# One add moves from VectorE to the head of GpSimd's string of adds

## The chip, the cores and the metric

The kernel runs on one core of a Trainium2 chip. The metric is the device time of one execution in microseconds (us), the median of three runs. Engine names in the profile: PE is TensorE's matrix product, PEld its weight load, DVE is VectorE, ACT is ScalarE, POOL is GpSimd, SP is SyncE, which here only issues transfers. L906 is line 906 of the kernel.

## What is computed

```python
# x: 8 x 4096 x 192, weight: 8 heads x 7 taps, w_in: 192 x 2048, w_out: 2048 x 192, all float32
w = softmax(weight)                                     # over the 7 taps of each head
idx = np.arange(S)[:, None] + np.arange(K)[None, :]
x_unf = x_pad[:, idx, :].reshape(B, S, K, H, group)     # x_pad: 6 zeros ahead of each sequence
x = np.einsum('hk,bskhg->bshg', w, x_unf).reshape(B * S, D)
h = x @ w_in
g = h * (1.0 / (1.0 + np.exp(-1.702 * h)))
out = g @ w_out
```

So each of the 32768 tokens gets a weighted sum of itself and its six predecessors (the convolution, seven taps), and then a two-layer network with the activation `g`.

## The kernel before, in words

**Chunks and periods.** The tokens are worked through in 32 chunks of 1024 (`N_BIG`), numbered `big`. After a first chunk of its own form, each chunk has a first product, conv(x) @ w_in (function `hidden`, line 775), and a second product, g @ w_out (function `second`, line 1154). I call one first product with the second product behind it a period. Both products use a scheme in which sums and differences of blocks are multiplied instead of the blocks themselves, so that fewer products are needed and many adds are. In the trace, TensorE's matmuls of the first product stand at L709 (164 of them in a period, 41 terms of four) and those of the second at L1172 (some 624).

**The order is written by hand.** `HIDDEN` (line 737) is a list of steps of the first product, `PLAN` (line 1108) one of the second. A program walks through a list and issues each step at once; the step goes to the end of its engine's queue. Each engine works through its queue in order and waits by semaphore where an operand isn't ready or a place is still being read. So the place of a step in the list decides what it stands behind on its own engine. In `HIDDEN`, "mm" is a term on TensorE, "copy" and "gelu" move or activate a bank of results (engine "a" is ScalarE, "v" VectorE), "join" adds two results on VectorE, "tap" makes the next tap on ScalarE, "add" adds taps, "over", "ve", "vl" make sums of convolved blocks on GpSimd (L435, L437) and "vc", "over" and "vl" issue their copies across the two halves of the partitions on SP (L609). In `PLAN`, "go" issues matmuls, "join" adds on VectorE (L435, L437), "turn" transposes a finished result on VectorE (L1091), and "acc" is an accumulating transfer issued by GpSimd (L1148).

**The taps.** The convolution of a chunk is made ahead, from the second product two chunks before to the first product one chunk before. Its 192 columns form three groups c = 0, 1, 2. From the fourth chunk on, ScalarE makes all 21 taps (line 570): `x` shifted by k, times weight k, 128 x 512 values each, every one into a place of its own (`tap_home`), k = 0 straight into the sum's place (`own`). The places are parts of buffers that are free just then, mostly of `g`. Taps 1 and 5 of group 2 use the same place, as do taps 3 and 6. The list "ready" holds the taps in the order c = 1, 0, 2; eighteen are issued in `PLAN`, the last three (c = 2, k = 4, 5, 6) in `HIDDEN`, of which k = 4 stands at the very start of the first product.

**The adds of the taps.** The taps of groups 0 and 1 are summed by accumulating transfers on GpSimd's queue (L595), with four last adds on GpSimd, "fin 0" to "fin 3". Those of group 2 are summed by six adds of 128 x 512 values, "c2 1" to "c2 6"; the number is that of the tap that is added. In `tap`, line 572 chooses what a tap is added to:

```python
base = tap_home(big, c, 2) if k in (3, 4) else dst
```

So taps 3 and 4 are added to tap 2, and tap 2 with both, tap 1, tap 5 and tap 6 to the sum. The step ("add", engine, name) in `HIDDEN` issues one of them if its tap has been made (line 906 for either engine). GpSimd's queue holds, in order: "c2 1", "fin 0", "fin 1", "fin 2", "c2 2", "fin 3", "c2 5", "c2 6", and then the sums of "vl" 19, "over", "ve" 0 and "vl" 15. VectorE's queue holds "c2 3" between two pairs of copies out of PSUM and "c2 4" behind the second pair. "c2 2" waits for "c2 4". This is done in 29 of the periods.

Of the kernel before, what the change touches and what calls it, by code (L numbers as in the profile page):

```python
# [15 lines left out]
def kernel(  # L16
# [101 lines left out]
    g = consts.tile([P, NG, 2, 2, NG, T], F32)  # L118
# [80 lines left out]
    def own(big):  # L199
        return conv_t[:, big % 2 * NR : big % 2 * NR + NR, :]  # L200
# [156 lines left out]
    for c in range(NC):  # L357
        part = sel[:, c, :].rearrange("i (h q) -> i h q", h=2)
        for sign in (1, -1):
# [5 lines left out]
                base=R * c if sign == 1 else group - 1 - R * c,  # L365
# [170 lines left out]
    def tap_home(big, c, k):  # L536
        if big == 1:
            return homes_1[c][k - 1]
        if big < 3:
            return (first_taps if c == 0 else taps[3])[k - 1]  # L540
        return taps[c][k - 1]

    def conv_src(big, c, k, ns=slice(0, 2)):
        return xts[big][:, c, ns, Q - PAD + k : Q - PAD + k + T]

    def conv(big, c, k, ns=slice(0, 2), times=vec.tensor_scalar_mul):
        src = conv_src(big, c, k, ns)
        dst = own(big)[:, 2 * c + ns.start : 2 * c + ns.stop, :]
        tap = cw[:, c, k : k + 1]
        if k == 0:  # L550
            times(dst, src, tap)
        else:
            vec.scalar_tensor_tensor(
                out=dst, in0=src, scalar=tap, in1=dst, op0=ALU.mult, op1=ALU.add
            )
# [10 lines left out]
    def tap(big, c, k):  # L566

        dst = own(big)[:, 2 * c : 2 * c + 2, :]
        home = tap_home(big, c, k) if k else dst
        act.mul(home, conv_src(big, c, k), cw[:, c, k : k + 1])  # L570
        if k and c not in DMA_TAPS and big > 2:
            base = tap_home(big, c, 2) if k in (3, 4) else dst
            to_add[f"c{c} {k}"] = base, home
            add_homes(big, c, k)
            return
        if big > 2:
            add_homes(big, c, k)
            if (c, k) == (0, K - 1):
                for i, (b, j, n) in enumerate(FINAL):
                    out, src = (tap_home(big, b, q) if q else own(big)[:, 2 * b : 2 * b + 2, :] for q in (j, n))  # L580
                    to_add[f"fin {i}"] = out, src
            return
        homes = [dst] + [tap_home(big, c, i) for i in range(1, K)]
        for a, b in (PAIRS_1 if big == 1 and c == 0 else TREE).get(k, ()):
            tree.append((homes[a], homes[b]))
        end_taps(2 if big == 2 and (c or k == K - 1) else 0)
# [3 lines left out]
    def add_homes(big, c, k):  # L590
        for b, i, j in LATER.get((c, k), ()) if big > 2 else ():
            out, src = (
                tap_home(big, b, n) if n else own(big)[:, 2 * b : 2 * b + 2, :] for n in (i, j)
            )
            nc.gpsimd.dma_start(out=out, in_=src, accum_op=ALU.add)  # L595

    def end_taps(left=0):
        while len(tree) > left:
            out, src = tree.pop(0)
            nc.gpsimd.dma_start(out=out, in_=src, accum_op=ALU.add)  # L600
# [96 lines left out]
    def prepare_taps(big):  # L697

        for c in (0, 2) if big < 3 else (1, 0, 2):
            for k in range(K):  # L700
                yield "", 1.0, lambda c=c, k=k: tap(big, c, k)
        yield f"taps {big}", 0.0, lambda: None
# [29 lines left out]
    def plain(u, m, n, v, slot, ks=range(NC), first=0):  # L732
# [2 lines left out]
            product1(slot, NC * (2 * u + m) + k, 2 * k + n, 0, v, k == first)  # L735

    HIDDEN = [
# [693 lines left out]
    for big in range(1, N_BIG):  # L1431
        more = big + 1 < N_BIG
        hidden(big, tiles, work)
        f, x, a, y = (tiles[i] for i in NEXT)
# [37 lines left out]
```

## Time and profile before

| | us |
|---|---|
| median of 3 runs (2297.59 to 2299.92) | 2299.07 |
| the profiled execution, its own time | 2295.66 |
| its span, from the first to the last instruction | 2293.9 |
| TensorE busy | 2258.6 |
| VectorE busy | 2158.2 |
| ScalarE busy | 1715.2 |
| GpSimd busy | 919.4 |

The busy times are those of the span of 2293.9. The granted clock of TensorE is 0.999 of full speed over the span. In the rows of the profile, "room<-room,slot" names the output's tile and then the inputs' tiles; `slot` and `sums` lie in PSUM, all others in SBUF (`out_dram` and `in_x_dram` in HBM). "96x256" is partitions by elements. In a timeline a row gives start and length in us, the engine, the line, the operation, and in brackets the engine's idle time before it and what ended that. In the waits a row gives who waited for whom, the total, the times and the longest. Rows of several equal instructions are merged (x2).

### The profile page before, as it was taken

The numbers are of one execution on the slowest core, as the hardware profiler recorded it, in microseconds if no ns is written. First come the engines' busy times: TensorE is split into PE (matmuls) and PEld (weight loads), VectorE is DVE, ScalarE is ACT, GpSimd is POOL, SyncE is SP. The second block draws the span as 40 slices with busy tenths as digits, with TensorE's granted clock in tenths as the row PEclk, the third lists the DMA queues.
The fourth block names the chain that finished last, engine by engine and source line by source line (L and its number), as shares of the span: only waits on it lengthen the run. The fifth ranks groups of instructions, "written<-read, shape, count | busy, mean of one in ns | idle before, by whom it ended". The sixth has DMA issues, their size and how long they took to land.

```text
span 2293.9 us, 63896 instructions
## 1 busy us (share of the span) xinstructions
PE 2258.6 (98%) x25090; PEld 1342.3 (59%) x25090; DVE 2158.2 (94%) x3297; ACT 1715.2 (75%) x3335; POOL 919.4 (40%) x980
## 2 busy tenths in 40 slices
PE   9999999999999999999999999999999999999999
PEld 5356566656566756666555555555555555657754
DVE  8999999999999999999999999999999999999998
ACT  8767777777877777777777677777777777777744
POOL 1534444334543344443345433354334444334510
PEclk9999999999999999999999999999999999999999
DMA  9986678766778767787666876668866768765643
GB/s 203 160 171 141 136 143 161 154 129 141 142 155 160 141 135 146 142 163 151 134 140 131 161 158 137 133 137 157 162 140 134 148 134 166 153 134 112 136 97 70
DMA packets 341995, 329.66 MB, mean 144 GB/s; under 512 B 131648, under 2 KB 280768, under 8 KB 341696
## 3 DMA queue, kind: packets, MB, share of 16 engines
q0 software_dynamic: 66352, 167.47, 41.4%
q1 hardware_dynamic: 273696, 157.72, 30.0%
q8 instruction: 199, 3.26, 0.6%
q14 instruction: 100, 0.82, 0.1%
q10 hardware_dynamic: 1648, 0.39, 0.1%
HBM read 53.15 MB, written 25.17 MB: 34 GB/s over the span
## 4 chain that ended last, share of the span: by engine, by line
PE 86%; DVE 7%; DMA 3%; issue 2%; ACT 2%; POOL 0%; SPq 0%; ACTq 0%; DVEq 0%; POOLq 0%
PE slot L709 34%; PE slot L1172 25%; PE sums L1172 15%; PE sums L709 12%; DVE room L435 2%; DVE room L437 1%; DVE g L437 1%; DMA w_form<-w_form 1%; DVE osbs L1091 1%; DMA g<-g 1%; DMA w_out_s<-w_form 0%; DMA g<-osbs 0%; ACT room L1201 0%; ACT room L1197 0%; DMA w_form<-w_out_s 0%
## 5 line engine op out<-in xcount | busy, mean ns | idle before, releaser
L709 PE MATMUL slot<-conv_t,w_in_s 64*128 64x512 f32 x3372 | 865.7, 593 | 4.3 <-DMA conv_t<-conv_t 1.4
L1172 PE MATMUL slot<-g,w_form 128*32 128x256 f32 x5872 | 716.9, 379 | 0.4 <-ACT slot L1201 0.4
L709 PEld LDWEIGHTS slot<-conv_t,w_in_s 64*128 64x128 f32 x3372 | 455.3, 187 | 295.7 <-issue 182.4
L437 DVE TENSOR_TENSOR g<-g 128x1024 f32<-128x1024 f32 x372 | 443.5, 1219 | 25.2 <-ACT g L833 18.4
L1172 PE MATMUL sums<-g,w_form 128*32 128x256 f32 x3800 | 422.2, 379 | 0.0
L1172 PEld LDWEIGHTS slot<-g,w_form 128*32 128x32 f32 x5872 | 362.1, 110 | 90.6 <-ACT slot L1201 0.9
L709 PE MATMUL sums<-conv_t,w_in_s 64*128 64x512 f32 x1284 | 379.5, 592 | 0.6 <-DMA conv_t<-conv_t 0.3
L826 ACT ACTIVATE g<-slot 128x512 f32<-128x512 f32 x494 | 266.2, 624 | 124.9 <-PE slot L709 124.6
L1172 PE MATMUL slot<-g,w_out_s 128*32 128x256 f32 x4080 | 321.8, 380 | 22.0 <-DVE room L435 20.9
L1197 ACT COPY room<-slot 32x256 f32<-32x256 f32 x434 | 158.9, 366 | 212.5 <-PE slot L1172 203.2
L1148 POOL DMA_DIRECT2D g<-g x124 | 116.0, 936 | 455.1 <-PE slot L1172 348.9
L906 POOL TENSOR_TENSOR conv_t<-conv_t,g 128x512 f32<-128x512 f32 x174 | 229.2, 1333 | 132.5 <-DVE g L906 105.0
L437 POOL TENSOR_TENSOR conv_t<-conv_t 128x256 f32<-128x256 f32 x210 | 181.8, 882 | 235.1 <-PE slot L709 89.6
L570 ACT ACTIVATE g<-xt,cw 128x512 f32<-128x512 f32 x389 | 270.3, 719 | 4.4
L1172 PEld LDWEIGHTS slot<-g,w_out_s 128*32 128x32 f32 x4080 | 164.1, 110 | 154.2 <-DVE room L435 30.1
L1172 PEld LDWEIGHTS sums<-g,w_form 128*32 128x32 f32 x3800 | 210.8, 110 | 69.7
L709 PEld LDWEIGHTS sums<-conv_t,w_in_s 64*128 64x128 f32 x1284 | 176.8, 187 | 108.3 <-issue 66.0
L833 ACT ACTIVATE g<-g 128x1024 f32<-128x1024 f32 x155 | 170.2, 1098 | 2.0 <-DVE g L817 1.9
L709 PE MATMUL slot<-g,w_in_s 64*128 64x512 f32 x556 | 170.6, 591 | 0.2 <-DVE slot L817 0.2
L1197 ACT COPY room<-sums 32x256 f32<-32x256 f32 x217 | 79.5, 366 | 105.4 <-PE sums L1172 95.9
L826 ACT ACTIVATE g<-sums 128x512 f32<-128x512 f32 x188 | 104.5, 615 | 58.4 <-PE sums L709 57.6
L1172 PE MATMUL sums<-g,w_out_s 128*32 128x256 f32 x1872 | 146.0, 380 | 0.1
(243 smaller groups left out, 3895.0 us busy)
## 6 DMA issues: line engine op xcount, KB each, us to landing
g<-g POOLq DMA_DIRECT2D x124, 512.0 KB, 6.5
conv_t<-conv_t SPq DMA_DIRECT2D x844, 64.0 KB, 2.0
xin<-in_x_dram SPq DMA_DIRECT2D x240, 180.0 KB, 6.4
out_dram<-osbs SPq DMA_DIRECT2D x186, 128.0 KB, 2.5
g<-g POOLq DMA_DIRECT2D x66, 256.0 KB, 6.5
g<-g SPq DMA_DIRECT2D x248, 64.0 KB, 3.5
g<-room POOLq DMA_DIRECT2D x31, 512.0 KB, 6.1
g<-osbs POOLq DMA_DIRECT2D x30, 512.0 KB, 6.4
```

The costliest lines, as they stand in the source:

```text
L435: eng.tensor_add(v(dst), v(a), v(b))
L437: eng.tensor_sub(v(dst), v(a), v(b))
L570: act.mul(home, conv_src(big, c, k), cw[:, c, k : k + 1])
L709: nc.tensor.matmul(slot[h], w_in_s[halves[h], a, v * P : (v + 1) * P], src, start=first, stop=True, skip_group_check=True,)
L826: act.activation(dst[:, :, h, :], ot(bank(src, h)), AF.Gelu_apprx_sigmoid, scale=float(sign))
L833: act.activation(dst.rearrange("p o h t -> p h o t"), src, AF.Gelu_apprx_sigmoid, scale=float(sign))
L906: (vec if eng == "v" else nc.gpsimd).tensor_add(dst, dst, home)
L1091: vec.transpose(osb[:, n, js, m * Q : (m + 1) * Q], src)
L1148: nc.gpsimd.dma_start(out=spot(dst), in_=spot(a), accum_op=ALU.add)
L1172: nc.tensor.matmul(dst, w, t, start=first, stop=last, skip_group_check=True)
L1197: act.copy(to, d)
```

## The change

Two places of the kernel are edited. Tap 4 of group 2 is now added to tap 1, no longer to tap 2; and this add goes from VectorE to GpSimd and stands in `HIDDEN` right behind the step in which ScalarE makes tap 4, ahead of "c2 1". The sum is that of the same seven taps.

```diff
         if k and c not in DMA_TAPS and big > 2:
-            base = tap_home(big, c, 2) if k in (3, 4) else dst
+            base = tap_home(big, c, {3: 2, 4: 1}[k]) if k in (3, 4) else dst
             to_add[f"c{c} {k}"] = base, home
...
     HIDDEN = [
-        ("mm", 0, 8, 1, 1), ("tap",), ("add", "g", "c2 1"), ("add", "g", "fin 0"), ("add", "g", "fin 1"),
-        ("mm", 0, 0, 2, 1), ("copy", "a", "k0", "p1", 1), ("mm", 0, 2, 3, 1), ("copy", "v", "k4", "p0", 1),
-        ("copy", "a", "k5", "p2", 1), ("mm", 0, 16, 1, 0), ("add", "v", "c2 3"), ("add", "g", "fin 2"),
-        ("copy", "a", "k6", "p3", 1), ("mm", 1, 13, 0, 0), ("copy", "v", "k2", "p1", 1), ("mm", 0, 3, 2, 0),
-        ("copy", "a", "k3", "p0", 1), ("add", "v", "c2 4"), ("mm", 0, 13, 3, 0), ("copy", "v", "k1", "p2", 1),
+        ("mm", 0, 8, 1, 1), ("tap",), ("add", "g", "c2 4"), ("add", "g", "c2 1"), ("add", "g", "fin 0"),
+        ("add", "g", "fin 1"), ("mm", 0, 0, 2, 1), ("copy", "a", "k0", "p1", 1), ("mm", 0, 2, 3, 1),
+        ("copy", "v", "k4", "p0", 1), ("copy", "a", "k5", "p2", 1), ("mm", 0, 16, 1, 0), ("add", "v", "c2 3"),
+        ("add", "g", "fin 2"), ("copy", "a", "k6", "p3", 1), ("mm", 1, 13, 0, 0), ("copy", "v", "k2", "p1", 1),
+        ("mm", 0, 3, 2, 0), ("copy", "a", "k3", "p0", 1), ("mm", 0, 13, 3, 0), ("copy", "v", "k1", "p2", 1),
         ("add", "g", "c2 2"), ("add", "g", "fin 3"), ("copy", "a", "p0", "k6", -1), ("mm", 0, 6, 1, 0),
```

The number and the order of all other steps stay as they are. On GpSimd's queue the string becomes "c2 4", "c2 1", "fin 0", "fin 1", "fin 2", "c2 2", "fin 3", "c2 5", "c2 6", with "c2 4" waiting for ScalarE's tap 4; "c2 2" now waits for "c2 3" alone.

## The prediction

> **What bounds the kernel now.** I read the page first, for which engine is full, then TensorE's waits, then a table of whole periods, and last the rows of each engine around the one wait that counts.
>
> ```profile
> span 2293.9 us, 63896 instructions
> PE 2258.6 (98%) x25090; PEld 1342.3 (59%) x25090; DVE 2158.2 (94%) x3297; ACT 1715.2 (75%) x3335; POOL 919.4 (40%) x980
> ```
> ```profile
> PE slot L1172 <- DVE room L435: 20.9, 19, 1.3
> ```
> TensorE is busy for 98% of the span and VectorE for 94%; GpSimd has room. Nothing that leaves TensorE's work alone can bring much more than TensorE's own gaps. In the waits of PE one line stands out: 19 waits of about 1.1 us (20.9 in all) for an add of VectorE in the second product. How much time such a wait costs is seen from periods. A period runs from one chunk's first product to the next; the table of windows has 28 periods together, the one period before them, three first products alone, and two whole periods (columns: length, busy time and instructions of each engine, granted clock, share of the DMA engines, GB/s).
>
> ```profile
> 248.92:2219.54 1970.62, 1950.86 (x22068) 1174.57 (x22064) 1864.68 (x2798) 1487.66 (x2894) 821.85 (x863) 1.00 0.72 143
> 177.55:248.92 71.37, 70.07 (x792) 47.18 (x788) 67.95 (x100) 53.96 (x104) 31.22 (x33) 1.00 0.75 149
> 600.62:636.26 35.64, 35.64 (x169) 19.50 (x165) 34.25 (x52) 28.46 (x52) 16.77 (x17) 1.00 0.55 122
> 951.47:987.11 35.64, 35.64 (x168) 26.79 (x164) 34.45 (x52) 28.47 (x52) 17.14 (x18) 1.00 0.52 117
> 530.59:566.81 36.22, 36.22 (x168) 26.17 (x165) 35.40 (x52) 29.11 (x53) 16.57 (x17) 1.00 0.55 122
> 882.03:951.47 69.44, 69.44 (x792) 44.04 (x788) 65.57 (x100) 53.45 (x104) 28.37 (x31) 1.00 0.74 148
> 1022.20:1092.96 70.76, 69.66 (x792) 47.86 (x788) 67.34 (x101) 53.45 (x104) 29.39 (x32) 1.00 0.73 146
> ```
> A period without a gap takes 69.44 us, with TensorE busy from end to end at the full clock (1.00). One with the gap takes 70.76, 1.32 more. So 69.44 is the floor and the change can only win the gaps. Where the 1.32 comes from is in the timeline ahead of the first product that starts at 1022.20 (start, length, engine; then VectorE, GpSimd and TensorE in turn):
>
> ```profile
> 1017.17 0.42 DVE L435 TENSOR_TENSOR room<-room 96x256 f32<-96x256 f32 x1
> 1017.51 2.11 DVE L437 TENSOR_TENSOR room<-room 96x256 f32<-96x256 f32 x1
> 1019.55 0.43 DVE L1091 STREAM_TRANSPOSE osbs<-room 96x256 f32<-96x256 f32 x1
> 1019.91 0.37 DVE L435 TENSOR_TENSOR room<-room,slot 96x256 f32<-96x256 f32 x1
> ```
> ```profile
> 1017.16 0.86 POOL L595 DMA_DIRECT2D conv_t<-g  x1 [2.35 <-DMA g<-g]
> 1017.73 1.60 POOL L906 TENSOR_TENSOR conv_t<-conv_t,g 128x512 f32<-128x512 f32 x1
> 1020.03 1.28 POOL L906 TENSOR_TENSOR conv_t<-conv_t,g 128x512 f32<-128x512 f32 x1 [0.70 <-DMA g<-room]
> 1021.27 2.64 POOL L906 TENSOR_TENSOR g<-g 128x512 f32<-128x512 f32 x2
> ```
> ```profile
> 1018.89 0.38 PE L1172 MATMUL slot<-g,w_form 128*32 128x256 f32 x1
> 1020.34 0.42 PE L1172 MATMUL slot<-g,w_out_s 128*32 128x256 f32 x3 [1.07 <-DVE room L435]
> ```
> A subtraction of VectorE with both inputs in SBUF (room<-room), whose like takes 0.42, takes 2.11: it ends at 1019.62, 0.29 after GpSimd's add (1017.73 + 1.60 = 1019.33). That add is "c2 1", GpSimd's first of the period. Everything behind on VectorE is 1.7 us late, the join room<-room,slot among it, which TensorE then awaits until 1020.34. Beside it the same place of the clean period that begins at 882.03:
>
> ```profile
> 878.63 0.42 DVE L437 TENSOR_TENSOR room<-room 96x256 f32<-96x256 f32 x1
> ```
> ```profile
> 879.19 1.61 POOL L906 TENSOR_TENSOR conv_t<-conv_t,g 128x512 f32<-128x512 f32 x1
> ```
> Here "c2 1" starts 0.14 after the subtraction has ended, nothing is held, and no gap follows. So the gap is a collision: an add of GpSimd holds a VectorE operation whose inputs are both in SBUF.
>
> **The change part by part.** What moves is GpSimd's whole string of adds. Its new first member, "c2 4", needs the tap that ScalarE makes at the head of the first product:
>
> ```profile
> 1022.75 0.72 ACT L570 ACTIVATE g<-xt,cw 128x512 f32<-128x512 f32 x1
> ...
> 1028.81 1.33 ACT L570 ACTIVATE g<-xt,cw 128x512 f32<-128x512 f32 x2
> ```
> The first row is that tap (k=4), done at 1023.47; the second is taps 5 and 6. GpSimd works in order, so "c2 1", "fin 0" and "fin 1" behind "c2 4" cannot start before 1023.5. Between 1018 and 1023.5 GpSimd then has no add to run, and the subtraction at 1017.51 has nobody to be held by. That removes the gap in each of the 19 periods that have it.
>
> The sum of that, from the windows: 28 periods take 1970.62 against 28 x 69.44 = 1944.32, so 26.3 us lie above the floor. The period before them (71.37) ends with such a gap too, worth 1.3 by the longest wait: 27.6 together. Some 25 of it are the 19 gaps (19 x 1.32 = 25.1), the rest are late starts in the first product. These have the same origin: the last join, room<-room at 1023.15, is held by "fin 2" (GpSimd's second add of the row at 1021.27):
>
> ```profile
> 1023.15 1.04 DVE L435 TENSOR_TENSOR room<-room 96x256 f32<-96x256 f32 x1
> ...
> 1025.77 0.67 DVE L906 TENSOR_TENSOR g<-g 128x512 f32<-128x512 f32 x1
> ```
> After the change it starts at the same 1023.15 (it follows TensorE's last product), takes 0.42 and is over at 1023.57, about when "c2 4" begins. VectorE's two copies and its remaining add "c2 3" come 0.6 us earlier, "c2 3" at about 1025.1.
>
> What the change adds, first on VectorE. "c2 4" (0.67) goes, but "c2 3" has both inputs in SBUF and now meets GpSimd: "c2 4" runs from 1023.5 to 1024.8, "c2 1" from 1024.8 to 1026.1. So "c2 3" is held until about 1026.1 and ends near 1026.6 instead of 1026.4. The trace has this case already:
>
> ```profile
> 954.60 1.46 DVE L906 TENSOR_TENSOR g<-g 128x512 f32<-128x512 f32 x1
> ```
> ```profile
> 603.52 1.46 DVE L906 TENSOR_TENSOR g<-g 128x512 f32<-128x512 f32 x1
> ```
> In these two periods "c2 3" took 1.46 instead of 0.67, asked for 3.1 after the first product's start at 951.47 and 2.9 after that at 600.62, and both first products still took 35.64. The cover is that TensorE wants the banks that VectorE copies out only some time later. Where the cover fails is the first product of 530.59:
>
> ```profile
> 534.32 1.45 DVE L906 TENSOR_TENSOR g<-g 128x512 f32<-128x512 f32 x1
> ```
> There "c2 3" came 3.7 after the start, 0.8 later than at 600.62, was held as long, and the product took 36.22. The new hold thus costs between 0 and 0.58 a period, 0 to 16.2 over 28. I take 1.1 us in all, near the lower end, since my timeline (the last join free, "c2 3" asked for 2.9 after the start) is that of 600.62.
>
> Then on GpSimd. The nearest rows for the added operation are its own kind on both engines:
>
> ```profile
> L906 POOL TENSOR_TENSOR g<-g x58: 1263/1276/1609, 179.2 to 2151.9; 128x512 f32<-128x512 f32 x58
> L906 DVE TENSOR_TENSOR g<-g x58: 667/674/1462, 181.1 to 2155.4; 128x512 f32<-128x512 f32 x58
> ```
> One more add of 1.28 (1.61 at most) on GpSimd for 0.67 on VectorE. By the Trainium skill (GPSIMD Engine Reference, Engine selection) an elementwise add of two tensors belongs on VectorE, GpSimd being about twice as slow; the two medians here (1.276 and 0.674) agree. By that rule the move loses time; what it would make of this kernel is the third rival.
>
> The string now has nine adds back to back from 1023.5, some 1.27 each, and a pause of up to 0.5 while "c2 3" reads: it ends at about 1035.4. Before it ended here:
>
> ```profile
> 1028.31 5.10 POOL L906 TENSOR_TENSOR conv_t<-conv_t,g 128x512 f32<-128x512 f32 x4 [4.40 <-DVE g L906]
> 1033.36 0.73 POOL L437 TENSOR_TENSOR g<-conv_t 128x256 f32<-128x256 f32 x1
> 1034.05 0.74 POOL L435 TENSOR_TENSOR conv_t<-conv_t 128x256 f32<-128x256 f32 x1
> 1034.87 2.11 POOL L437 TENSOR_TENSOR conv_t<-conv_t 128x256 f32<-128x256 f32 x3
> 1040.03 0.73 POOL L437 TENSOR_TENSOR conv_t<-conv_t 128x256 f32<-128x256 f32 x1 [3.05 <-issue]
> ```
> So the five sums behind (blocks 19, 12 twice, 13, 15) move back by 2.0 us, and the wait of 3.05 ahead of 1040.03 swallows that: from there on nothing moves. SP copies those blocks across the halves, 2.0 us from issue to landing, so the last is there by about 1041.5 rather than 1039.5; behind them on SP stand copies of later sums, which do not move.
>
> ```profile
> conv_t<-conv_t SPq DMA_DIRECT2D x844, 64.0 KB, 2.0
> ```
> ```profile
> 1048.91 2.99 PE L709 MATMUL slot<-conv_t,w_in_s 64*128 64x512 f32 x12
> ```
> The first term that reads block 15 is the 33rd of 41 at 0.86 each, in this row of TensorE, at 1049.7. Room: 8 us.
>
> There are two new orders to keep. ScalarE's tap 5 overwrites the place that "c2 1" reads, so it now waits for "c2 1": ready at 1026.1 to 1026.6, tap at 1028.81, room 2.2. Behind that tap on ScalarE stand copies that TensorE needs, so this is the first place where a late string would be felt. And the adds after "c2 1" have no wait for ScalarE other than the ones they had.
>
> Sum: 27.6 - 1.1 = 26.5 us. The profiled execution took 2295.66 (span 2293.9 and 1.8 around it) and would take 2269.2. The median of the timed runs is 3.4 higher, 2299.07; the gain applied to it gives **2272.6**.
>
> **The rivals.** *The collision moves into the first product.* "c2 3", or a later join of two SBUF operands, is held longer than I reckon, and TensorE waits there in every period, as at 530.59. For it: VectorE's add and GpSimd's string now always overlap. Against it: the first products of 600.62 and 951.47 had that overlap and took 35.64. At the full 0.58 a period it gives back 16.2 of the 27.6: 2287.7; in part, 2276 to 2287.
>
> *The gap stays.* If the subtraction was late for another reason than "c2 1" (the DMA issue at 1017.16, say, which remains), the 19 gaps remain: about 2299. Against it: it ended 0.29 after the add, not after the issue (1018.02), and in the clean period no hold goes with an add that comes later.
>
> *GpSimd's string becomes the path (slower).* Place: the end of the nine adds, first felt at ScalarE's tap 5 and then at blocks 19 and 15. If the 2.0 us by which it ends later were on the path in each of 28 periods, they would cost 56 against 26.5 to 27.6 won: about 2328. It decides once "c2 1" ends over 2.2 us later than I reckon, or block 15 over 8; to end slower than before the string has to be some 3.2 later (2.2 and 1.0 more, 28 x 1.0 being the gain). For it: 40% of busy time on GpSimd is an average, and every one of its waits is for someone. Against it: the 3.05 of idle time behind the string, and adds never over 1.61. It is the case that the rule named above would give.
>
> **How the numbers follow.** Forecast 0.75; collision moved 0.13; gap stays 0.05; string on the path 0.07. A measurement of this kernel can tell about 0.2%, 4.6 us, from no change, so faster means below 2294.5: the first two cases, 0.88; same 0.05; slower 0.07. The range: the lower end is the lowest timed run with all 27.6 taken off, 2297.59 - 27.6 = 2270.0, less 1.5 for what the floor may hide: 2268.5. The upper end takes in the moved collision: 2288. The two remaining cases, 0.12, are left out.
>
> **What would show it.** In the profile of the changed kernel: the line PE slot L1172 <- DVE room L435 gone or down to a few tenths; L437 room<-room never at 2 us; GpSimd's first L906 add of each period starting 1.3 us after the first product instead of up to 4.8 before it; "c2 3" on VectorE at 1.3 to 1.5 in nearly all of 29 periods and the first product still 35.64; GpSimd's 3.05 wait down to about 1; periods of 69.44 throughout. I am wrong if the first product grows (first rival), if the second product keeps its gap (second), or if ScalarE is seen waiting for GpSimd at L570 or TensorE for a transfer into conv_t (third).

## The result, and the profile after

The changed kernel takes 2269.55 us (median of 4 runs, 2267.85 to 2270.92) against 2299.49 of the kernel before (also 4 runs, 2297.59 to 2301.35). The ratio is 0.9869, with a 95% interval of 0.9852 to 0.9887: 26 to 34 us less. The profiled execution took 2267.85 instead of 2295.66, 27.8 less, and its trace shows where they came from. The page first:

```profile
span 2266.1 us, 63896 instructions
PE 2251.1 (99%) x25090; PEld 1345.5 (59%) x25090; DVE 2114.3 (93%) x3268; ACT 1710.6 (75%) x3335; POOL 985.0 (43%) x1009
```

The span is 27.8 shorter, TensorE's busy time only 7.5. The 29 adds that moved are the 29 instructions that VectorE has less and GpSimd more; VectorE's busy time fell by 44 us, though 29 adds of 0.67 are 20. The rest is a balance: an operation that stands still counts as busy, and the room<-room ones at L435 and L437 take 89.5 us in all where they had taken 138.5, while others take more, above all slot<-room,osbs at L817 (89.7 instead of 65.5). In the waits of PE the line for L435 with its 19 waits is gone; this is the top of the list now:

```profile
PE slot L709 <- ACT slot L802: 2.4, 2, 1.5
PE slot L709 <- DVE slot L817: 2.0, 2, 1.7
```

The windows show the 28 periods from the second on, and one first product:

```profile
247.29:2191.74 1944.45, 1944.45 (x22069) 1183.17 (x22065) 1823.59 (x2769) 1483.69 (x2894) 887.94 (x893) 1.00 0.73 145
...
1011.25:1046.89 35.64, 35.64 (x169) 22.00 (x166) 33.87 (x51) 28.34 (x52) 20.66 (x19) 1.00 0.52 116
```

1944.45 / 28 = 69.44: every period has the length that only the clean ones had before, and TensorE is busy in all of it. Here is the place of the old gap, on GpSimd and then on VectorE; the first product starts at 1011.25.

```profile
1007.01 0.86 POOL L595 DMA_DIRECT2D conv_t<-g  x1 [2.47 <-DMA g<-g]
1012.61 1.27 POOL L906 TENSOR_TENSOR g<-g 128x512 f32<-128x512 f32 x1 [4.74 <-ACT g L570]
1013.96 3.22 POOL L906 TENSOR_TENSOR conv_t<-conv_t,g 128x512 f32<-128x512 f32 x2
```
```profile
1007.50 0.42 DVE L435 TENSOR_TENSOR room<-room 96x256 f32<-96x256 f32 x1
1007.84 0.41 DVE L437 TENSOR_TENSOR room<-room 96x256 f32<-96x256 f32 x1
...
1012.19 0.38 DVE L435 TENSOR_TENSOR room<-room 96x256 f32<-96x256 f32 x1
...
1014.15 0.67 DVE L906 TENSOR_TENSOR g<-g 128x512 f32<-128x512 f32 x1
```

GpSimd issues its transfer at 1007.01, beside the same operations of VectorE as before, and then has 4.74 us without work: it waits for ScalarE's tap 4. In that time VectorE's two room<-room operations take 0.42 and 0.41 where the second had taken 2.11, and the last join at 1012.19 takes 0.38 where it had taken 1.04. "c2 4" starts at 1012.61, 1.36 after the first product.

One thing is not as forecast: "c2 3" on VectorE (1014.15) was not held. It took 0.67, and GpSimd's "c2 1" behind 1013.96 was the one to wait. All 29 pairs went that way; of GpSimd's adds into conv_t the longest took 2.0:

```profile
L906 POOL TENSOR_TENSOR conv_t<-conv_t,g x174: 1253/1274/2006, 180.6 to 2134.7; 128x512 f32<-128x512 f32 x174
...
L906 DVE TENSOR_TENSOR g<-g x29: 664/666/668, 180.7 to 2125.3; 128x512 f32<-128x512 f32 x29
```

### The profile page after: what moved, and what is told of

It is laid out like the page before. It is cut to its first block, busy times and chain, and to the rows that moved or that the text cites. A ratio compares the mean times of both kernels' runs of the same rounds, so it can differ in the third digit from the quotient of the medians.

```text
span 2266.1 us, 63896 instructions
## 1 busy us (share of the span) xinstructions
PE 2251.1 (99%) x25090; PEld 1345.5 (59%) x25090; DVE 2114.3 (93%) x3268; ACT 1710.6 (75%) x3335; POOL 985.0 (43%) x1009
## 4 chain that ended last, share of the span: by engine, by line
PE 96%; issue 1%; DMA 1%; SPq 1%; DVE 1%; ACT 0%; POOL 0%; DVEq 0%; POOLq 0%; ACTq 0%
PE slot L709 37%; PE slot L1172 28%; PE sums L1172 17%; PE sums L709 13%; PE slot L980 2%; DMA xin<-in_x_dram 0%; SPq L99 0%; DMA osbs<-room 0%; SPq L1102 0%; POOL conv_t L437 0%; DVE xt L518 0%; DVE g L435 0%; ACT conv_t L1278 0%; DVE conv_t L437 0%; POOL g L1148 0%
## 5 line engine op out<-in xcount | busy, mean ns | idle before, releaser
L709 PE MATMUL slot<-conv_t,w_in_s 64*128 64x512 f32 x3372 | 823.6, 593 | 3.5 <-ACT slot L802 2.4
L709 PEld LDWEIGHTS slot<-conv_t,w_in_s 64*128 64x128 f32 x3372 | 449.8, 187 | 287.9 <-issue 175.0
L437 DVE TENSOR_TENSOR g<-g 128x1024 f32<-128x1024 f32 x372 | 443.5, 1219 | 10.8 <-ACT g L833 1.9
L709 PE MATMUL sums<-conv_t,w_in_s 64*128 64x512 f32 x1284 | 346.7, 592 | 0.9 <-DMA conv_t<-conv_t 0.6
L437 POOL TENSOR_TENSOR conv_t<-conv_t 128x256 f32<-128x256 f32 x210 | 195.4, 948 | 152.4 <-PE slot L709 90.3
L906 POOL TENSOR_TENSOR conv_t<-conv_t,g 128x512 f32<-128x512 f32 x174 | 238.6, 1393 | 4.5
L709 PEld LDWEIGHTS sums<-conv_t,w_in_s 64*128 64x128 f32 x1284 | 171.1, 187 | 106.2 <-issue 56.2
L906 POOL TENSOR_TENSOR g<-g 128x512 f32<-128x512 f32 x87 | 110.7, 1273 | 121.9 <-ACT g L570 119.6
L709 PE MATMUL slot<-g,w_in_s 64*128 64x512 f32 x556 | 149.7, 593 | 1.7 <-DVE slot L817 1.7
```

Source lines behind the costliest of these rows:

```text
L437: eng.tensor_sub(v(dst), v(a), v(b))
L709: nc.tensor.matmul(slot[h], w_in_s[halves[h], a, v * P : (v + 1) * P], src, start=first, stop=True, skip_group_check=True,)
L906: (vec if eng == "v" else nc.gpsimd).tensor_add(dst, dst, home)
```

## The experiments

The theory to test is the **collision**: GpSimd's early "c2 1" holds VectorE's joins with both inputs in SBUF at the end of the second product, and what counts is only when GpSimd's string starts. Its rival is **relief**: VectorE, busy for 94%, had one add too many, and the add's departure is what counts. The change does both things at once, so the first two kernels do one each. Times are medians; "over the floor" is the time of the 28 periods less 28 x 69.44 = 1944.3, which leaves out what happens before the second period (its start varied by up to 4.7 us between the profiles, 247.3 to 252.0). Each ratio is to runs of the kernel before that were made together with the experiment (medians 2298.78 to 2300.23).

**The order alone.** GpSimd's string begins with "c2 4" as in the change, and VectorE keeps two adds, "c2 1" in place of "c2 4".

```diff
-            base = tap_home(big, c, 2) if k in (3, 4) else dst
+            base = tap_home(big, c, {3: 2, 4: 1}[k]) if k in (3, 4) else dst
...
-        ..., ("tap",), ("add", "g", "c2 1"), ("add", "g", "fin 0"), ...
+        ..., ("tap",), ("add", "g", "c2 4"), ("add", "g", "fin 0"), ...
...
-        ..., ("add", "v", "c2 4"), ...
+        ..., ("add", "v", "c2 1"), ...
```

> GpSimd's string begins with c2 4 (into tap 1) as in the change, but VectorE keeps two adds: c2 1 takes the place of c2 4 on it. The collision theory (c2 1 of GpSimd holds VectorE's joins at the end of the second product, and a string that waits for ScalarE's tap 4 can't) expects the whole gain, about 2270 us, periods of 69.45 and no wait of PE for L435. The relief theory (VectorE, busy for 94%, had one add too many) expects no gain, about 2299.

It took 2272.78 us, ratio 0.9885 (0.9868 to 0.9901). There is no line for L435 room in PE's waits. Its 28 periods, and VectorE's adds in it:

```profile
251.12:2198.17 1947.05, 1947.05 (x22068) 1157.10 (x22064) 1838.67 (x2797) 1487.55 (x2894) 835.11 (x865) 1.00 0.73 145
```
```profile
L906 DVE TENSOR_TENSOR g<-g x29: 665/667/670, 184.5 to 2131.5; 128x512 f32<-128x512 f32 x29
L906 DVE TENSOR_TENSOR conv_t<-conv_t,g x29: 1537/1540/1550, 186.5 to 2133.6; 128x512 f32<-128x512 f32 x29
```

2.7 over the floor instead of 26.3: the order alone brings nine tenths of the gain. The remaining 0.1 a period lies in the first product, 35.73 instead of 35.64: VectorE's second add now runs beside the string, is held in every period (1.54 instead of 0.67), and the copies behind it come later. That TensorE waits for these copies is likely but not shown: the profile has TensorE busy throughout.

**The move alone.** "c2 4" goes to GpSimd, but behind "fin 2".

```diff
-        ..., ("add", "v", "c2 3"), ("add", "g", "fin 2"),
+        ..., ("add", "v", "c2 3"), ("add", "g", "fin 2"), ("add", "g", "c2 4"),
...
-        ..., ("copy", "a", "k3", "p0", 1), ("add", "v", "c2 4"), ...
+        ..., ("copy", "a", "k3", "p0", 1), ...
```

> c2 4 goes from VectorE to GpSimd, but behind fin 2, so that the string still begins with c2 1 ahead of the first product. The collision theory expects the gaps to stay in some 19 periods: 2296 to 2300 us. The relief theory expects the gain, about 2270.

2298.87 us, ratio 0.9999 (0.9989 to 1.0008). All gaps are there:

```profile
PE slot L1172 <- DVE room L435: 20.8, 19, 1.3
```

So VectorE's relief by itself is worth nothing that can be measured, and the relief theory falls.

**"c2 1" behind the "fin" adds.** The kernel before, with nothing moved between engines; only "c2 1" gives up its place at the head.

```diff
-        ..., ("tap",), ("add", "g", "c2 1"), ("add", "g", "fin 0"), ...
+        ..., ("tap",), ("add", "g", "fin 0"), ...
...
-        ..., ("add", "g", "fin 2"),
+        ..., ("add", "g", "fin 2"), ("add", "g", "c2 1"),
```

> The kernel before with one edit: c2 1 stands behind fin 2 on GpSimd, and nothing moves between engines. fin 0 waits for a transfer and starts about 1 us before the first product at the earliest, when VectorE's joins with both inputs in SBUF are over but for the last one. The collision theory expects the gap in the second product to vanish (24 us less), the last join and c2 3 to be held as in the period of 530.59, and so some tenths lost in many first products: 2272 to 2287 us. The relief theory expects no gain, 2299.

2278.29 us, ratio 0.9907 (0.9890 to 0.9923). The line for L435 room is down to one wait, and what is left is in the first products. The last two rows show VectorE in the longest of them, which starts at 1573.46:

```profile
PE slot L1172 <- DVE room L435: 0.5, 1, 0.5
```
```profile
248.88:2201.90 1953.02, 1952.80 (x22068) 1254.32 (x22065) 1848.49 (x2797) 1493.16 (x2894) 812.26 (x865) 1.00 0.73 145
```
```profile
1574.40 1.41 DVE L435 TENSOR_TENSOR room<-room 96x256 f32<-96x256 f32 x1
...
1577.39 1.45 DVE L906 TENSOR_TENSOR g<-g 128x512 f32<-128x512 f32 x1
```

8.7 over the floor, 0.4 of it in a second product and the rest in first products of 35.64 to 36.43. This is the loss that the prediction's first rival feared: the last join is held (1.41 instead of 0.38), then "c2 3" too (1.45 instead of 0.67), and the first product takes longer, though the profile counts TensorE as busy in it. The adds "fin 0" to "c2 1" run on across the start of the first product here; a string that begins 1.36 after it is late enough for the last join.

**"c2 1" early, all others late.** The counterpart: "c2 1" stays at the head, and "c2 4", added to the sum itself by GpSimd, stands second and makes the rest wait for tap 4.

```diff
-            base = tap_home(big, c, 2) if k in (3, 4) else dst
+            base = tap_home(big, c, 2) if k == 3 else dst
...
-        ..., ("add", "g", "c2 1"), ("add", "g", "fin 0"), ...
+        ..., ("add", "g", "c2 1"), ("add", "g", "c2 4"), ("add", "g", "fin 0"), ...
...
-        ..., ("copy", "a", "k3", "p0", 1), ("add", "v", "c2 4"), ...
+        ..., ("copy", "a", "k3", "p0", 1), ...
```

> VectorE is relieved of c2 4, which GpSimd adds to the sum itself, second in its string and waiting for tap 4; c2 1 stays first and early. So only c2 1 can meet the joins of the second product, and all other adds begin in the first product. The collision theory expects the gaps to stay in full and only the late starts in the first product to go: 2293 to 2297 us. The relief theory expects about 2270.

2295.06 us, ratio 0.9980 (0.9970 to 0.9989).

```profile
PE slot L1172 <- DVE room L435: 23.3, 21, 1.3
```
```profile
248.19:2218.88 1970.69, 1948.49 (x22069) 1078.13 (x22065) 1842.30 (x2770) 1484.72 (x2894) 870.66 (x892) 1.00 0.72 143
```

21 gaps, all in second products; no first product is over 35.65. The late starts of the first products are gone (2.4 us in the 28 periods of the kernel before), but there are two gaps more, so that the 28 periods take as long as before (1970.69 and 1970.62). The ratio's 0.2% therefore isn't found in this profile, and its cause stays open. With the run before it this fixes the culprit: "c2 1" alone in its early place makes the gaps, and without it there one wait of 0.5 is left.

**Tap 4 to tap 2 again.** The changed kernel with its first edit undone.

```diff
-            base = tap_home(big, c, {3: 2, 4: 1}[k]) if k in (3, 4) else dst
+            base = tap_home(big, c, 2) if k in (3, 4) else dst
```

> The changed kernel with the first of its two edits undone: tap 4 is added to tap 2 again, by GpSimd at the head of its string, and c2 3 on VectorE (into tap 2 as well) now waits for it. The collision theory sees only the start of the string and expects the changed kernel's time, 2268 to 2272 us: c2 4 ends 2.6 us after the first product's start, c2 3 is asked for at 2.9. If c2 3 is held longer here than in the changed kernel (there GpSimd was the one that waited), some tenths a period are lost: up to 2280.

2269.06 us, ratio 0.9875 (0.9860 to 0.9890): the changed kernel's time. Here it is "c2 3" that is held, as the prediction had it for the change:

```profile
1016.07 2.95 POOL L906 TENSOR_TENSOR conv_t<-conv_t,g 128x512 f32<-128x512 f32 x2
```
```profile
1016.37 1.52 DVE L906 TENSOR_TENSOR g<-g 128x512 f32<-128x512 f32 x1
```

(the first row is GpSimd's "c2 1" and "fin 0") and the first product around it still takes 35.64, as they all do. (One second product of the 28 periods is 0.7 longer; TensorE waits there for an operation at L437, not for one of these.) So whichever of the two waits at this place, it costs nothing, and the choice of the tap to add to doesn't matter.

**Both adds on GpSimd.** The changed kernel with "c2 3" on GpSimd as well.

```diff
-        ..., ("add", "v", "c2 3"),
+        ..., ("add", "g", "c2 3"),
```

> The changed kernel with VectorE's last add, c2 3, on GpSimd too, ahead of fin 2: ten adds in the string, none on VectorE; ScalarE's tap 6 now waits for c2 3. The collision theory with TensorE as the floor expects no change, 2268 to 2271 us, because the string's end has room. The rule that an add costs twice as much on GpSimd, with the string as the path, expects 28 times 0.6 to 1.3 us more: 2287 to 2306.

2269.10 us, ratio 0.9877 (0.9862 to 0.9891), its 28 periods at the floor with ten adds in the string:

```profile
248.23:2192.73 1944.50, 1944.50 (x22068) 1088.86 (x22065) 1813.22 (x2741) 1487.52 (x2894) 907.63 (x921) 1.00 0.73 145
```
```profile
ACT g L570 <- POOL g L906: 11.0, 29, 0.4
```

The new wait is there, 0.4 in every period: ScalarE's tap 6 waits for "c2 3", which reads tap 3 from the same place, as the prediction's third rival had it for tap 5 and "c2 1". It has room; nothing follows from it. The Trainium skill puts an elementwise add of two tensors on VectorE, GpSimd being about twice as slow (GPSIMD Engine Reference, Engine selection). Read as a rule for this kernel, that would make both moves cost time. An add did take 1.27 instead of 0.67, as the page has it, but neither the changed kernel nor this one is slower for it: the string's end isn't on the path.

**"c2 1" in halves.** The kernel before, with "c2 1" as two adds of 128x256 one after the other.

```diff
-                (vec if eng == "v" else nc.gpsimd).tensor_add(dst, dst, home)
+                parts = [slice(0, 1), slice(1, 2)] if what == "c2 1" else [slice(0, 2)]
+                for o in parts:
+                    (vec if eng == "v" else nc.gpsimd).tensor_add(dst[:, o, :], dst[:, o, :], home[:, o, :])
```

> The kernel before with c2 1 as two adds of 128x256 instead of one of 128x512, in the same early place. If VectorE is held for one instruction of GpSimd, it is held about half as long (some 0.7 to 1.0 instead of 1.7 us), and the 19 gaps of 1.3 shrink to 0.3 to 0.6: 2281 to 2288 us. If it is held for as long as GpSimd has adds to do, nothing changes: 2299. The relief theory expects 2299 too.

No gain: 2301.05 us, ratio 1.0012 (1.0003 to 1.0022), the second of the two cases that were expected. GpSimd and VectorE in a period with the gap (the edit moves later lines by two):

```profile
1092.67 0.86 POOL L595 DMA_DIRECT2D conv_t<-g  x1 [1.95 <-DMA g<-g]
1093.24 1.74 POOL L908 TENSOR_TENSOR conv_t<-conv_t,g 128x256 f32<-128x256 f32 x2
```
```profile
1093.05 2.21 DVE L435 TENSOR_TENSOR room<-room 96x256 f32<-96x256 f32 x1
```

VectorE did not get in between the halves: its operation ends at 1095.26, 0.28 after the second one (1093.24 + 1.74 = 1094.98). That it is held for one instruction of GpSimd is wrong, then, at least for two short ones back to back.

**One half early.** The first half in the old place, the second behind "fin 0", which waits for a transfer.

```diff
-        ..., ("add", "g", "c2 1"), ("add", "g", "fin 0"), ...
+        ..., ("add", "g", "c2 1", 0), ("add", "g", "fin 0"), ("add", "g", "c2 1", 1), ...
...
-        def add(eng, what):
+        def add(eng, what, o=None):
...
-                dst, home = to_add.pop(what)
+                dst, home = to_add[what] if o == 0 else to_add.pop(what)
+                if o is not None:
+                    dst, home = dst[:, o, :], home[:, o, :]
```

> The kernel before with c2 1 in two adds of 128x256, the first in the old early place, the second behind fin 0, which waits for a transfer. So GpSimd runs one short add where it ran two back to back in the run with the halves together. If VectorE is held for as long as GpSimd's adds follow each other without a pause, the hold is about 0.7 us shorter than there (1.0 instead of 1.7) and the 19 to 21 gaps shrink from 1.3 to about 0.6: 2283 to 2288 us. If VectorE is held for a fixed time by whatever add comes right after GpSimd's transfer issue, the gaps stay: 2299.

2287.31 us, ratio 0.9950 (0.9932 to 0.9967).

```profile
PE slot L1174 <- DVE room L435: 11.8, 21, 0.7
```
```profile
1154.83 0.86 POOL L595 DMA_DIRECT2D conv_t<-g  x1 [2.21 <-DMA g<-g]
1155.39 1.06 POOL L908 TENSOR_TENSOR conv_t<-conv_t,g 128x256 f32<-128x256 f32 x1
```
```profile
1154.96 1.77 DVE L435 TENSOR_TENSOR room<-room 96x256 f32<-96x256 f32 x1
```

The hold ends 0.28 after GpSimd's run here too (1154.96 + 1.77 = 1156.73 against 1156.45). The waits of TensorE follow the length of that run: one of 1.74 gives 26.0 / 21 = 1.24 a gap (the line below, of the run with the halves together), one of 1.60 gives 20.9 / 19 = 1.10, one of 1.06 gives 11.8 / 21 = 0.56.

```profile
PE slot L1174 <- DVE room L435: 26.0, 21, 1.4
```

In all three the run is 0.5 us longer than the wait: that much costs TensorE nothing, and between these three each tenth of a microsecond more on GpSimd is a tenth more of waiting on TensorE.

## Why the prediction was right, point by point

- **The gain of 27.6 to the floor.** The 28 periods fell from 1970.62 to 1944.45, 26.2 where the working had 26.3. The period before them fell from 71.37 to 69.44, 1.9 where 1.3 was reckoned (the gap was 1.5, and its first product lost 0.4 as well). The start came 0.3 later. 26.2 + 1.9 - 0.3 = 27.8, the whole difference of the profiled executions. The working's split of the 26.3 was somewhat off, which its sum doesn't feel: of the 19 waits one lies in the period before, so the 28 periods have 18, and late first products cost 2.4 in them where the working left 1.2.
- **The price of the new overlap, 1.1.** It was 0. "c2 3" was to be held and wasn't; GpSimd was. The run with tap 4 added to tap 2 has the overlap as I had drawn it, and it costs nothing either. That the other end of the range (0.58 a period) was real is shown by the run with "c2 1" behind the "fin" adds, whose first products reach 36.43. In that run a first product takes 35.64 where "c2 3" ends within 4.6 us of its start, and from there it grows as "c2 3" ends later (at 5.4 in the longest). In the changed kernel "c2 3" ends at 3.6, with tap 4 to tap 2 at 4.4, which is where my timeline had it. The period of 951.47, with "c2 3" ending at 4.6 and a first product of 35.64, had already shown that this is free. So 1.1 is the mis-sized term; that it was small next to 27.6 is why the sum held although the overlap went the other way round.
- **The string's end.** Forecast 13.2 us after the first product's start, measured 13.5; "c2 1" waited 0.7 where a pause of up to 0.5 was reckoned. The five sums behind moved by 2.4 instead of 2.0, and GpSimd's wait of 3.05 behind them is gone rather than down to 1:

```profile
1024.76 0.73 POOL L437 TENSOR_TENSOR g<-conv_t 128x256 f32<-128x256 f32 x1
1025.44 0.73 POOL L435 TENSOR_TENSOR conv_t<-conv_t 128x256 f32<-128x256 f32 x1
1026.25 3.69 POOL L437 TENSOR_TENSOR conv_t<-conv_t 128x256 f32<-128x256 f32 x4
```

- **A new collision that I only hinted at.** Those sums now meet a later join of VectorE:

```profile
1026.11 1.28 DVE L817 TENSOR_TENSOR g<-slot,room 128x512 f32<-128x512 f32 x2
1027.31 2.05 DVE L817 TENSOR_TENSOR slot<-room,osbs 128x512 f32<-128x512 f32 x2
```

  Both rows run beside the same adds of GpSimd (1026.25 to 1029.94). The first has an input in PSUM (`slot`) and takes 0.64 apiece, not held; the second has both in SBUF and takes 2.05 for the two. In the kernel before GpSimd was idle beside that pair (in its wait of 3.05), and it took 1.28:

```profile
1038.39 1.28 DVE L817 TENSOR_TENSOR slot<-room,osbs 128x512 f32<-128x512 f32 x2
```

  The Trainium skill says the same of the pair (SBUF — State Buffer, Who interferes with whom): a VectorE instruction contends with a GpSimd one that reads SBUF if both its inputs lie in SBUF, and, outside VectorE's two-port modes, not if at most one does. The two rows agree. The first product stays at 35.64 all the same.
- **ScalarE's tap 5** came at 1017.85, 6.6 after the start as before; "c2 1" was done by 1015.95. The room was 1.9 where I had 2.2.
- **The sum.** 2272.6 was forecast from the median and 2269.55 measured. Of the 3.0 between, 1.1 is the overlap's price, 0.6 the first period, and 0.3 of the start goes the other way. The rest, 1.6, is less than the runs of one kernel differ among themselves (2267.85 to 2270.92). The measured time lies 1.0 above the lower end of the range.
- **The second rival,** that the transfer issue makes the gap, is out: in the changed kernel the issue (1007.01 to 1007.87) still falls beside the two room<-room operations at 1007.50 and 1007.84, and neither is held.

No kernel here beats the changed one. With tap 4 to tap 2, or with both adds on GpSimd, the time is the same: all three have their 28 periods within 0.8 us of the floor. That 69.44 is a floor is read from the traces, where none of the 29 periods of any of these kernels is shorter but the last one (69.3). A busy TensorE doesn't prove it, since the order alone shows it busy throughout as well at 69.53 a period. If it is one, more can come only from TensorE's own work or from what lies outside these periods.

## What to carry to other kernels

An add on a half-idle engine needn't be free beside a full one: before counting busy shares, look for operations in the same group with two lengths (0.42 and 2.11 here) and see what runs on GpSimd when the long one happens. The cure here was not to take work from the full engine but to move the other's work in time: make its string begin with something that can't be ready too early, and check that the later place has slack on the path. To tell order from load, build the two kernels that do one each.

## What the runs showed of the hardware that I had not expected

- Who is held doesn't follow from the starts in the trace. At the end of the second product VectorE's operation started first (1093.05 against 1093.24) and was held; in the first product GpSimd's add started first (1013.96 against 1014.15) and GpSimd was held; with GpSimd's start 0.1 further ahead (1016.07 against 1016.37, tap 4 to tap 2) VectorE was. The Trainium skill says that whichever starts first has the shared ports for the whole instruction (SBUF — State Buffer, SBUF: two separate sides); the starts that the profile gives do not show this order, and what decides was not found.
- Two adds of 128x256 back to back held VectorE through both (2.21), while in a string of longer adds it got its turn after one (tap 4 to tap 2: "c2 3" takes 1.52, and GpSimd's next add waits in turn, so that two take 2.95). What makes the difference was not tried.
- An add of 128x256 right behind a transfer issue shows 1.06 us, its like elsewhere 0.73, and one of 128x512 shows 1.60 instead of 1.27: some 0.33 more, in the length of the hold too. The two adds of 128x256 back to back seem to have it once: they take 1.74, where I estimate 1.41 for two without it, from the rows at 1024.76 and 1025.44 (0.68 from start to start, and 0.73 for the second).
